# Two dK stores of head pairs issued from GpSimd as sixteen transfers of 8 partitions each

## The chip, the cores and the metric

The kernel runs on one core of a Trainium2 chip. The metric is the device time of one execution in microseconds (us), median over runs; the kernel before takes 1698.33 us (three runs, 1697.89 to 1698.5). Five engines matter: PE (TensorE, matmuls and transposes into PSUM), DVE (VectorE), ACT (ScalarE), POOL (GpSimd) and SP (SyncE, which here only issues transfers). Sixteen DMA engines move data between device memory and the on-chip memory of 128 partitions. A transfer is issued either from SP, into the queue that the profile calls `q1 hardware_dynamic`, or from POOL, into `q0 software_dynamic`. All queues are served by the same sixteen DMA engines. A transfer counts as landed when all sixteen have reported.

## The reference, cut to what matters

The reference is the forward pass and the gradient of one decode step: layer norm, attention of one query token over a cache of 4096 keys and values (4 batches x 32 heads x 128 channels, bf16), an output projection, and a gated feed-forward block, with residuals. It returns the forward result and the gradients of eight inputs.

```python
def _A_ref(x, k_cache, v_cache, wq, wo):
    q = (x @ wq).reshape(B, Sq, H, Dh).transpose(0, 2, 1, 3)
    scores = jnp.einsum("bhqd,bhkd->bhqk", q, k_cache) * (Dh ** -0.5)
    p = _softmax(scores, axis=-1)
    o = jnp.einsum("bhqk,bhkd->bhqd", p, v_cache)
    return o.transpose(0, 2, 1, 3).reshape(B, Sq, H * Dh) @ wo
...
h = x + _A_ref(_layernorm(x, axis=-1), A_k_cache, A_v_cache, A_wq, A_wo)
h2 = h + _B_ref(_layernorm(h, axis=-1), B_w1, B_w3, B_w2)
...
_out, _vjp = jax.vjp(_f, A_x, A_k_cache, A_v_cache, A_wq, A_wo, B_w1, B_w3, B_w2)
_grads = _vjp(grad_out)
```

What fills the time is the cache and its gradients. With one query token, the gradient of a head's keys is an outer product: dK[k, :] = dS[k] q, with dS[k] = scale * p[k] (dO . V[k] - c). The gradient of its values is dV[k, :] = p[k] dO. Each of K, V, dK and dV is 128 heads of 1 MB (4096 x 128 bf16). V is read twice, once for the forward pass and once for dS.

## The kernel before

Memory. A large tile `arena` is cut into 23 slots of 8 KB per partition and a little more, one head (1 MB) each. `Slot` hands out one slot; `Slot2` hands out two neighbouring ones, a pair of 2 MB. `give()` puts slots back, at the point of the program where it is called; who gets a slot next waits on the chip until the transfers that used it have landed. `free` and `age` make the choice: the slot that was given back longest ago is taken first. Up to `side_done` only eight pairs (`NPAIR`) are handed out as pairs.

Stages. First a forward pass over all 128 heads, which loads K and V of each head. Then a short middle part (feed-forward block, its gradients). Then the gradients of the cache: 32 heads one by one (`grad_V`, `grad_K`), and the other 96 as 48 pairs, the loop `for t in range(NT)` at the end of the kernel. A pair is two heads of the same batch; `two_heads` lays its 2 MB out as 128 rows of 16 KB, one for each partition, 64 partitions for each head.

One turn `t` of that loop, in the order of the program:

- `load_pairs` issues the load of V for pair `t + 3` or further ahead (line 1280, on SP);
- `front_pair(t + 3)` transposes V on PE (line 1298), copies it back on ACT (line 1299), forms dO . V on PE (line 1313), and `dO_pair` makes a small stationary operand on POOL (line 1290);
- `more_V` makes dV of a pair some turns ahead: `P2_pair` on POOL (line 1376), the outer product on DVE (line 1379, in `outer_pair`), and the store to `out_3` from SP (line 1389, in `grad_pair`);
- `grad_pair(out_2, t, ...)` does the same for dK: one DVE outer product (line 1379) into a fresh pair of slots, one store of 2 MB from SP (line 1389), and `give()`;
- after an odd turn `group_dS_pair` makes dS for the next two pairs on DVE (lines 1326 and 1329);
- `side` does pieces of other work: the gradients of the weights, with stores from SP (lines 1072, 1119, 1135, 1146) and a few small transfers from POOL: `dqr_bf` (line 1028), four rows of `out_1` (line 1064), four rows of `grad_out` (line 1083), four rows of `out_0` (line 1111) and `O_sb` (line 1124).

Each engine works through its own list in this order and waits for the others by semaphores. The order is written out by hand; nothing is scheduled later. A DMA issue on SP or POOL waits in the list of its engine until its data are ready, and what stands behind it waits too.

Of the kernel before, what the change touches and what calls it, by code (L numbers as in the profile page):

```python
# [21 lines left out]
SP = 32  # L22
NPAIR = 8
OLD = 9


@with_exitstack
def kernel(
# [22 lines left out]
    nc = tc.nc  # L51
    P = nc.NUM_PARTITIONS
# [5 lines left out]
    Dh = A_k_cache.shape[3]  # L58
# [6 lines left out]
    SJ = Sk // P  # L65
# [50 lines left out]
    def age(i):  # L116
        return given["n"] - given.get(i, -NSLOT)
# [7 lines left out]
    class Slot:  # L125
        def __init__(self, name, src=free):
            self.i = src[0]
            if part["B"] and src is free:
                lone = sorted((i for i in free if i not in part["pairs"]), key=age, reverse=True)
                self.i = lone[0] if name in SIDE or lone and age(lone[0]) >= OLD else max(free, key=age)  # L130
            src.remove(self.i)
# [76 lines left out]
    for i in range(2):  # L208
        t = fcon.tile([P, 64], BF16, name=f"onesw{i}")
# [4 lines left out]
    def ones_window(col):  # L214
# [11 lines left out]
                          in_=rowg[:, None, :, None].to_broadcast([P, 4, 8, 4]))  # L226
# [586 lines left out]
    def grad_V(s):  # L813
        b, h = bh_of(s)
        gv = Slot("gv")
        outer(gv.heads(), P2s.pop(s), reps["rdo", s // REP][:, s % REP, :])
        nc.sync.dma_start(out=rows_of(out_3[b, h]), in_=gv.heads())
        if s > 1:
            gv.give()
        else:  # L820
            first_gv.append(gv)
# [143 lines left out]
    with ExitStack() as c2:  # L965
# [206 lines left out]
        def replicate(nm_, i0):  # L1172
            if i0 >= NH or (nm_, i0 // REP) in reps:
                return
            K_ = 8 * B if i0 < 8 * B else P
            rows = dOrows_bf if nm_ == "rdo" else qrows_bf
            ps = psrep.tile([P, REP, Dh], FP32, tag="rep", name="rep_ps")
            for i in range(REP):
                nc.tensor.matmul(ps[:, i, :], lhsT=ident_b[0:K_, i0 + i:i0 + i + 1].to_broadcast([K_, P]), rhs=rows[0:K_, :],
                                 start=True, stop=True)  # L1180
            rt = rep_bufs[nm_][i0 // REP % 2]
            nc.scalar.copy(out=rt, in_=ps[:])
            reps[nm_, i0 // REP] = rt
# [11 lines left out]
        def P_pairs(s):  # L1195
            if s < SP and s not in P2s:
                P2s[s] = bw3.tile([P, SJ, 2], BF16, tag="P2", name="P2")
                nc.gpsimd.tensor_copy(out=P2s[s][:], in_=P_all[:, s, :, None].to_broadcast([P, SJ, 2]))
# [69 lines left out]
        def two(t):  # L1268
            s = SP + t // B * 2 * B + t % B
            return s, s + B  # L1270

        def two_heads(ap, t):
            b, h = t % B, H0 + t // B * 2
            return ap[b, h:h + 2].rearrange("h (p j) d -> (h p) (j d)", p=P // 2)

        def load_pair():
            t = npv["next"]
            npv["next"] += 1
            pV[t] = Slot2()
            nc.sync.dma_start(out=pV[t].t[:, 0:2 * SJ * Dh], in_=two_heads(A_v_cache, t))  # L1280

        def load_pairs(t):
            while npv["next"] < NT and (npv["next"] <= t or len(V2s) + 2 * len(pV) < 6 and len(Slot2.choices()) > 1
                                          and -min(Slot2.choices())[0] >= OLD - 2):
                load_pair()
# [33 lines left out]
        def group_dS_pair(g):  # L1319
            T = rows.pop("T").rearrange("p jj (c z l u a) -> p z l a c u jj", c=4, z=2, l=2, u=4, a=2)  # L1320
            t = rows.pop("t")[:, 0:4 * SJ].rearrange("p (l j) -> p l j", l=2)
            t5 = t.rearrange("p l (c u jj) -> p l c u jj", c=4, u=4)
            for l in range(2):
                for a, s in enumerate(two(2 * g + l)):
                    r_ = slice(64 * a, 64 * (a + 1))
                    nc.vector.tensor_scalar(out=t5[r_, l], in0=T[r_, 0, l, a], scalar1=c_rep[r_, s:s + 1],  # L1326
                                            scalar2=scale, op0=ALU.subtract, op1=ALU.mult)
            pdS[g] = bw3.tile([P, 2, 2 * SJ, 2], BF16, tag="dS2", name="dS2", bufs=1)
            nc.vector.tensor_tensor(out=pdS[g][:], in0=t[:, :, :, None].to_broadcast([P, 2, 2 * SJ, 2]),
                                    in1=P_two(2 * g)[:, :, :, None].to_broadcast([P, 2, 2 * SJ, 2]), op=ALU.mult)  # L1330
# [3 lines left out]
        def P_two(t, n=2):  # L1334
            return Pp["s"].b(NT * 2 * SJ).rearrange("p (t j) -> p t j", j=2 * SJ)[:, t:t + n, :]
# [20 lines left out]
        def replicate_pair(nm_, q):  # L1356
            if q >= NT // B or (nm_, "p", q) in reps:
                return
            s = SP + q * 2 * B
            K_ = 8 * B if s + 2 * B <= 8 * B else P  # L1360
            rws = dOrows_bf if nm_ == "rdo" else qrows_bf
            ps = psrep.tile([P, REP, Dh], FP32, tag="rep", name="rep_ps")
            for i in range(REP):
                for a in range(2):
                    n = s + i + a * B
                    nc.tensor.matmul(ps[64 * a:64 * (a + 1), i, :], lhsT=ident_b[0:K_, n:n + 1].to_broadcast([K_, P // 2]),
                                     rhs=rws[0:K_, :], start=True, stop=True, tile_position=(0, 64 * a))
            rt = rep_bufs[nm_][(H0 + q) % 2]
            nc.scalar.copy(out=rt, in_=ps[:])
            reps[nm_, "p", q] = rt  # L1370

        def P2_pair(t):
            if t < NT and t not in pP2:
                P_rows(t // B)
                pP2[t] = P2b[t % 2]
                nc.gpsimd.tensor_copy(out=pP2[t], in_=P_two(t, 1)[:, 0, :, None].to_broadcast([P, 2 * SJ, 2]))  # L1376

        def outer_pair(dst, col2, row):
            nc.vector.tensor_tensor(  # L1379
                out=dst.rearrange("p (j r t) -> p j r t", r=Dh // 2, t=2),  # L1380
                in0=col2[:, :, None, :].to_broadcast([P, 2 * SJ, Dh // 2, 2]),
                in1=row.rearrange("p (r t) -> p r t", t=2)[:, None, :, :].to_broadcast([P, 2 * SJ, Dh // 2, 2]),
                op=ALU.mult,
            )

        def grad_pair(out_ap, t, col2, row):
            g_ = Slot2()
            outer_pair(g_.t[:, 0:2 * SJ * Dh], col2, row)
            nc.sync.dma_start(out=two_heads(out_ap, t), in_=g_.t[:, 0:2 * SJ * Dh])
            g_.give()  # L1390

        O0, S0, S1, L, LP = 2, 21, 35, 5, 3
        gvd = {"n": 2, "t": 0}
# [1 line left out]
        def more_V(upto):  # L1395
            while gvd["n"] < min(SP, upto):
                s = gvd["n"]
                P_pairs(s)
                replicate("rdo", s - s % REP)
                grad_V(s)  # L1400
                P_pairs(s + 1)
                P_pairs(s + 2)
                gvd["n"] += 1
                if s % REP == 2 and s + 2 < SP:
                    replicate("rdo", s + 2)
                elif s % REP == 2:
                    replicate_pair("rdo", 0)
                if s >= SP - 2:
                    P2_pair(s - SP + 2)
            while gvd["t"] < NT and SP + 2 * gvd["t"] + 2 <= upto:  # L1410
                t = gvd["t"]
                P2_pair(t)
                replicate_pair("rdo", t // B)
                grad_pair(out_3, t, pP2.pop(t), reps["rdo", "p", t // B][:, t % B, :])
                P2_pair(t + 1)
                gvd["t"] += 1
                if t % B == 2:
                    replicate_pair("rdo", t // B + 1)

        def lead_V(s):  # L1420
            return 8 - 2 * min(3, max(0, s - 64) // 16)
# [6 lines left out]
        def side(s):  # L1428
            if O0 <= s < S0:
                step("o")  # L1430
            if s >= S1:
                step("s", 2)
            elif s >= O0:
                step("q")
# [41 lines left out]
        for t in range(NT):  # L1476
            s = SP + 2 * t
            load_pairs(t + LP)
            if t % B == 2:
                replicate_pair("rq", t // B + 1)  # L1480
            if t + LP < NT:
                front_pair(t + LP, lambda: side(s))
            else:
                if t + LP == NT:
                    rows_out()
                    rows_T()
                side(s)
            more_V(s + 2 + lead_V(s))
            grad_pair(out_2, t, pdS[t // 2][:, t % 2], reps["rq", "p", t // B][:, t % B, :])
            if t % 2 == 1 and t + 1 < NT:  # L1490
                group_dS_pair((t + 1) // 2)
            side(s + 1)
        step("s", 400)

# [29 lines left out]
```

## Time and profile before

| what | value |
|---|---|
| time, median of 3 runs | 1698.33 us (1697.89 to 1698.5) |
| profiled execution: span | 1696.2 us |
| outside of the span (median less span) | 2.1 us |
| busy share of the span: PE, DVE, ACT, POOL | 73%, 73%, 57%, 20% |
| moved by DMA | 707.45 MB, mean 417 GB/s |
| of it by q1 (issued from SP) | 704.94 MB |
| of it by q0 (issued from POOL) | 0.10 MB in 416 packets |
| stores of pairs (line 1389) | 96 of 2 MB, median 27.9 us from issue to landing |
| loads of pairs (line 1280) | 48 of 2 MB, median 32.1 us |

The span runs from the first to the last instruction of the profiled execution; all times below count from its start. The busy rows give each engine's share in forty equal slices, in tenths. The DMA row is the mean over the sixteen DMA engines, so one engine alone gives 1/16, or 0.06. The trace also holds a record of each DMA packet: its start, its length in time, its bytes and its queue, but not the number of its engine. A packet of 4 bytes ends each engine's share of a transfer.

### The profile page before, as it was taken

To read this page: it belongs to the slowest core of one execution; us is meant where nothing else is said; L and a number is where in the kernel's file an instruction comes from. 1 tells how busy PE (TensorE), PEld (TensorE's weight loads), DVE (VectorE), ACT (ScalarE), POOL (GpSimd) and SP (SyncE) were. 2 spreads that over 40 slices of the span, in tenths; PEclk is the share of its full clock that TensorE was granted. 3 is DMA by queue.
4 is the path that set the end of the run, shared out by engine and by line. 5 is a ranking of instruction groups with operands and counts; after the bars stand their busy time and mean duration, and the time that the engine had idled before them with its cause. 6 is when DMAs were issued, how large, how long until landed. Compare 5 with 4: busy or idle time off the path is not lost.

```text
span 1696.2 us, 37839 instructions
## 1 busy us (share of the span) xinstructions
PE 1233.4 (73%) x16228; PEld 943.4 (56%) x16228; DVE 1234.4 (73%) x1198; ACT 959.5 (57%) x1490; POOL 336.9 (20%) x583
## 2 busy tenths in 40 slices
PE   5889888888888888877876755667665666766650
PEld 4777667666677666655655544444444444444440
DVE  5989999999998997667766466575665655655683
ACT  3555544454454544677665555666665666666650
POOL 1211222222222222222231121011210102011120
PEclk8999999999999999899898689886678777676675
DMA  9999999999999999999999999999999999999995
GB/s 401 424 424 424 424 424 424 424 424 423 416 423 406 424 414 397 395 414 425 425 425 429 428 429 428 429 430 429 429 429 428 418 430 429 422 418 425 415 429 230
DMA packets 81000, 707.45 MB, mean 417 GB/s; under 512 B 8748, under 2 KB 12984, under 8 KB 15296
## 3 DMA queue, kind: packets, MB, share of 16 engines
q1 hardware_dynamic: 80416, 704.94, 99.0%
q8 instruction: 127, 2.08, 0.5%
q14 instruction: 41, 0.34, 0.0%
q0 software_dynamic: 416, 0.10, 0.0%
HBM read 422.59 MB, written 282.34 MB: 416 GB/s over the span
## 4 chain that ended last, share of the span: by engine, by line
DMA 46%; DVE 9%; PE 3%; issue 2%; ACT 1%; DVEq 0%; POOL 0%; SPq 0%; ACTq 0%
DMA out_dram<-arena 43%; DVE arena L1379 7%; DMA arena<-in_A_v_cache_dram 3%; DVE arena L806 1%; PE M_ps L472 1%; DVE arena L457 1%; PE pt_w L601 0%; ACT arena L1299 0%; ACT Pn L436 0%; DVEq L1519 0%; PE kP_ps L482 0%; DVE dPr L1326 0%; PE pt_tps L1298 0%; PE gu_ps L873 0%; PE dn_ps L904 0%
## 5 line engine op out<-in xcount | busy, mean ns | idle before, releaser
L1299 ACT COPY arena<-pt_tps 128x1024 bf16<-128x1024 bf16 x384 | 369.8, 1023 | 232.3 <-PE pt_tps L1298 231.6
L1298 PE MATMUL pt_tps<-ident_b,arena 128*128 128x128 bf16 x3072 | 308.1, 272 | 204.7 <-DMA arena<-in_A_v_cache_dram 149.4
L1298 PEld LDWEIGHTS <-arena 128*128 128x128 bf16 x3072 | 263.9, 125 | 304.2 <-DMA arena<-in_A_v_cache_dram 172.8
L1379 DVE TENSOR_TENSOR arena<-arena 128x8192 bf16<-128x8192 bf16 x48 | 212.5, 4427 | 205.1 <-DMA out_dram<-arena 202.3
L472 PE MATMUL M_ps<-arena 128*128 128x130 bf16 x4096 | 285.1, 222 | 42.9 <-DMA arena<-in_A_v_cache_dram 42.2
L457 DVE TENSOR_TENSOR arena<-arena 128x4096 bf16<-128x4096 bf16 x128 | 292.5, 2285 | 23.9 <-POOL arena L453 23.9
L472 PEld LDWEIGHTS <-arena 128*128 128x128 bf16 x4096 | 251.9, 99 | 64.0 <-DMA arena<-in_A_v_cache_dram 57.2
L1379 DVE TENSOR_TENSOR arena<-dS,arena 128x8192 bf16<-128x8192 bf16 x48 | 212.3, 4424 | 73.0 <-DMA out_dram<-arena 73.0
L364 DVE STREAM_TRANSPOSE arena<-arena 128x512 f32<-128x512 f32 (+1 forms) x321 | 250.7, 797 | 0.0
L359 ACT COPY arena<-pt_tps 128x1024 bf16<-128x1024 bf16 x128 | 129.5, 1012 | 188.9 <-PE pt_tps L358 150.5
L1376 POOL COPY arena<-arena 128x128 bf16<-128x128 bf16 x48 | 55.3, 1153 | 492.3 <-ACT arena L1353 286.3
L370 POOL TENSOR_TENSOR W<-qrep,wmask 128x128 bf16<-128x128 bf16 x128 | 120.2, 939 | 85.6 <-PE S_ps L390 70.8
L801 ACT COPY arena<-pt_tps 128x1024 bf16<-128x1024 bf16 x128 | 121.7, 1025 | 26.1 <-PE pt_tps L800 24.8
L453 POOL COPY arena<-P_all 128x64 bf16<-128x64 bf16 x128 | 32.7, 255 | 412.8 <-ACT P_all L447 409.8
L806 DVE TENSOR_TENSOR arena<-dS,arena 128x4096 bf16<-128x4096 bf16 x32 | 73.2, 2293 | 35.0 <-DMA out_dram<-arena 34.7
L800 PE MATMUL pt_tps<-ident_b,arena 128*128 128x128 bf16 x1024 | 78.5, 229 | 27.1 <-ACT arena L801 27.1
L1313 PE MATMUL dP_ps<-arena 128*32 128x512 bf16 x768 | 85.7, 484 | 7.6 <-ACT arena L1299 7.3
L800 PEld LDWEIGHTS <-arena 128*128 128x128 bf16 x1024 | 67.2, 104 | 37.5 <-issue 35.9
L447 ACT COPY P_all<-pt_P 32x64 bf16<-32x64 bf16 x256 | 52.1, 204 | 53.6 <-PE pt_P L443 51.4
L806 DVE TENSOR_TENSOR arena<-P,arena 128x4096 bf16<-128x4096 bf16 x29 | 66.4, 2295 | 19.8 <-DMA out_dram<-arena 19.8
L358 PE MATMUL pt_tps<-ident_b,arena 128*128 128x128 bf16 x1024 | 80.1, 222 | 0.0
L482 PE MATMUL kP_ps<-arena,onesw 128*32 128x512 bf16 x1024 | 79.6, 388 | 0.0
(245 smaller groups left out, 1576.5 us busy)
## 6 DMA issues: line engine op xcount, KB each, us to landing
out_dram<-arena SPq DMA_DIRECT2D x96, 2048.0 KB, 27.9
arena<-in_A_v_cache_dram SPq DMA_DIRECT2D x160, 1024.0 KB, 15.9
arena<-in_A_k_cache_dram SPq DMA_DIRECT2D x128, 1024.0 KB, 15.3
arena<-in_A_v_cache_dram SPq DMA_DIRECT2D x48, 2048.0 KB, 32.1
out_dram<-arena SPq DMA_DIRECT2D x72, 1024.0 KB, 20.2
arena<-in_A_wq_dram SPq DMA_DIRECT2D x8, 1024.0 KB, 14.4
arena<-in_B_w_dram SPq DMA_DIRECT2D x8, 896.0 KB, 15.3
out_dram<-arena SPq DMA_DIRECT2D x6, 896.0 KB, 28.4
```

The lines of the kernel that those rows point to most:

```text
L359: nc.scalar.copy(out=KT[:, c * GW:(c + 1) * GW, :], in_=pt[:])
L364: nc.vector.transpose(out=KT[:, c * w_:(c + n) * w_], in_=Kn[:, c * w_:(c + n) * w_])
L370: nc.gpsimd.tensor_tensor(out=W[:, hl], in0=qrep[:, :, s:s + 1].to_broadcast([P, 4, 32]), in1=wmask[:, hl, None, :].to_broadcast([P, 4, 32 ...
L457: nc.vector.tensor_tensor(out=PK[:, :, 0:Dh].rearrange("p j (r t) -> p j r t", t=2), in0=Ks[s].heads().rearrange("p j (r t) -> p j r t", t=2),
L472: nc.tensor.matmul(hold["M"][:], lhsT=Vn[:, j, :], rhs=PK[:, j, :], start=(j == 0), stop=(j == SJ - 1))
L800: nc.tensor.transpose(pt[:, i, :], v[:, g * GW + i, :], ident_b[:])
L801: nc.scalar.copy(out=v[:, g * GW:(g + 1) * GW, :], in_=pt[:])
L806: nc.vector.tensor_tensor(out=dst.rearrange("p j (r t) -> p j r t", t=2), in0=col2[:, :, None, :].to_broadcast([P, SJ, Dh // 2, 2]), in1=r ...
L1298: nc.tensor.transpose(pt[:, i, :], v[:, g * GW + i, :], ident_b[:])
L1299: nc.scalar.copy(out=v[:, g * GW:(g + 1) * GW, :], in_=pt[:])
L1313: nc.tensor.matmul(rows["acc"][32 * c:32 * (c + 1), :], lhsT=zt[t % B][:, 32 - m:64 - m], rhs=v[:, j0:j0 + 4, :], start=(pl == 0 and u == ...
L1379: nc.vector.tensor_tensor(out=dst.rearrange("p (j r t) -> p j r t", r=Dh // 2, t=2), in0=col2[:, :, None, :].to_broadcast([P, 2 * SJ, Dh / ...
```

## The change

A constant names two pairs, `t` = 30 and `t` = 38. For these, `grad_pair` of dK no longer issues its store from SP. It puts sixteen entries into a list `drips`. `drip(4)` takes up to four entries and issues each as a transfer of its own from POOL: 8 partitions, four apart, within a block of 32 (the first is partitions 0, 4, 8, ..., 28; the second 1, 5, ..., 29; the fifth begins the block at 32). Each transfer carries 8 rows of 16 KB, 128 KB in all. `drip(4)` is called twice in each turn, before and after `grad_pair` of dK, and does nothing when the list is empty. So the sixteen go out as four in the turn of the pair itself, eight in the next turn, and four in the one after; the pair's slots are given back after the last. DVE's outer product for the two pairs stays as it is, and so do all other transfers.

```diff
+SPLIT = (30, 38)
...
         def grad_pair(out_ap, t, col2, row):
             g_ = Slot2()
             outer_pair(g_.t[:, 0:2 * SJ * Dh], col2, row)
-            nc.sync.dma_start(out=two_heads(out_ap, t), in_=g_.t[:, 0:2 * SJ * Dh])
-            g_.give()
+            if out_ap is out_2 and t in SPLIT:
+                for r in range(P // 8):
+                    drips.append((two_heads(out_ap, t), g_, r))
+            else:
+                nc.sync.dma_start(out=two_heads(out_ap, t), in_=g_.t[:, 0:2 * SJ * Dh])
+                g_.give()
+
+        drips = deque()
+
+        def drip(n):
+            while drips and n:
+                dst, g_, r = drips.popleft()
+                r_ = slice(r // 4 * 32 + r % 4, r // 4 * 32 + 32, 4)
+                nc.gpsimd.dma_start(out=dst[r_], in_=g_.t[r_, 0:2 * SJ * Dh])
+                if r == P // 8 - 1:
+                    g_.give()
+                n -= 1
...
             more_V(s + 2 + lead_V(s))
+            drip(4)
             grad_pair(out_2, t, pdS[t // 2][:, t % 2], reps["rq", "p", t // B][:, t % B, :])
             if t % 2 == 1 and t + 1 < NT:
                 group_dS_pair((t + 1) // 2)
+            drip(4)
             side(s + 1)
```

## The prediction

> **What bounds the kernel now.** I read the page first: the DMA row, the queues, the chain, the issues.
>
> ```profile
> DMA  9999999999999999999999999999999999999995
> GB/s 401 424 424 424 424 424 424 424 424 423 416 423 406 424 414 397 395 414 425 425 425 429 428 429 428 429 430 429 429 429 428 418 430 429 422 418 425 415 429 230
> q1 hardware_dynamic: 80416, 704.94, 99.0%
> q8 instruction: 127, 2.08, 0.5%
> q0 software_dynamic: 416, 0.10, 0.0%
> DMA 46%; DVE 9%; PE 3%; issue 2%; ACT 1%; DVEq 0%; POOL 0%; SPq 0%; ACTq 0%
> out_dram<-arena SPq DMA_DIRECT2D x96, 2048.0 KB, 27.9
> ```
>
> The sixteen DMA engines are busy in every slice but the last; no other engine passes 73%. The change moves no byte fewer, so it can matter only by which DMA engine carries what, and by waits. The last slice is the interesting one: 230 GB/s. The busy times by stretch, cut around the end (length, then PE, PEld, DVE, ACT, POOL, then granted clock, DMA share, GB/s), and the packets of the last 17 us:
>
> ```profile
> 1640.00:1670.00 30.00, 8.63 (x84) 6.37 (x84) 26.68 (x11) 8.20 (x9) 3.50 (x1) 0.61 1.00 428
> 1670.00:1674.00 4.00, 0.00 (x0) 0.00 (x0) 0.00 (x0) 0.00 (x0) 0.00 (x0) 0.50 1.03 438
> 1674.00:1677.50 3.50, 0.00 (x0) 0.00 (x0) 0.00 (x0) 0.00 (x0) 0.00 (x0) 0.50 0.42 178
> 1677.50:1694.50 17.00, 0.00 (x0) 0.00 (x0) 0.00 (x0) 0.00 (x0) 0.00 (x0) 0.50 0.06 26
> DMA packets 31, 0.44 MB, mean 26 GB/s; under 512 B 4, under 2 KB 4, under 8 KB 4
> ```
>
> From 1677.5 to 1694.5 the share is 0.06, one engine of sixteen: 27 packets of 16 KB, one after another, while fifteen engines have nothing left. So the end is set by one late DMA engine, 17 us behind the rest, and not by the mean. The completion events say the same: the last store of a pair, issued at 1666.8, is reported by the first engine after 7.8 us, by the fifteenth after 10.8, by the last after 28.1. The gap between the fifteenth and the last report was 1.7 us for a transfer issued at 831, 8.3 at 1106, 13.8 at 1384, 17.3 at the end: one engine falls back steadily.
>
> **Which engine is late.** The packet records don't name engines, but they can be chained: a busy engine starts its next packet 3 to 4 ns before the recorded end of the last, and all sixteen run through the same list of q1 packets. Chained back from the end to 1119 us this gives sixteen complete lanes. The late lane has no hole; its 16 KB packets are 0.624 us apart on average from 1390 on, the others' 0.613 to 0.618 (0.607 undisturbed). The 24 packets of q8 in that time fall three each on eight lanes, never on the late one. So the lanes are two sets of eight, and the late lane is in the set without q8.
>
> **Where POOL's small transfers go.** q0 has 416 packets for 13 transfers, 32 each. In the stretch of the four-row store of `out_1` (line 1064):
>
> ```profile
> q0 software_dynamic: 32, 0.00, 2.1%
> ```
>
> Its records are 4 packets of 1 KB and 28 of 4 bytes: sixteen completions, and twelve fillers on the engines that got no row. So a transfer with fewer than sixteen rows still goes to all sixteen, one row each to the first engines, and 4 bytes to the rest. In the chained lanes the rows of all three late four-row transfers (`out_1`, `grad_out`, `out_0`) lie on the same four lanes. The first two transfers of the kernel, four rows each, show the same by another way: the 2 KB packets of both start 0, 21, 54 and 136 ns apart, modulo the 306 ns beat of the 8 KB packets around them. It does not rotate. And the four lanes are in the set without q8: the set of the late lane.
>
> [...]
>
> **The change, part by part.** *Removed:* two SP stores, 8 rows of 16 KB per engine each, so 16 rows on every engine. *Added:* 32 POOL transfers of 8 rows. By the above each puts one row on the first eight engines: 32 rows on each of these, none on the other eight. Net: +16 rows on eight engines, -16 on eight.
>
> If four rows take four lanes of the set without q8, I take it that eight rows take all eight of that set. Then the late engine gets 16 rows more: 16 x 0.62 = +9.9 us. Completions: 32 of 9 ns on each engine, less two, +0.3 us. Sum +10.2 us, all on the path, since the late lane has no hole to hide it in. The other seven of the set get 9.9 us too, but are 17 us early.
>
> Price of a row: from 0.607 (+9.7) up. The 1 KB rows of q0 took 42 to 43 ns from start to the next start, no surcharge over their length of 46, so I take none. The far end is a row of q8: its 16 KB packets took 0.88 to 0.97 us instead of 0.61; at +0.33 for each of 32 rows, 10.6 us more. The q0 row is the nearer, being a store of the same queue; I keep some of the far end above.
>
> *POOL.* The relevant rows (mean ns; then idle before):
>
> ```profile
> L1028 POOL DMA_DIRECT2D arena<-dqr_bf x4 | 2.2, 561 | 9.3 <-ACT dqr_bf L1024 9.3
> L1376 POOL COPY arena<-arena 128x128 bf16<-128x128 bf16 x48 | 55.3, 1153 | 492.3 <-ACT arena L1353 286.3 <-DVE arena L1379 205.9
> POOL arena L1376 <- ACT arena L1353: 92.4, 3, 31.5
> DVE arena L1379 <- DMA out_dram<-arena: 76.2, 21, 6.8
> ```
>
> An issue costs 0.56 us, eight in a turn 4.5 us. The copy of line 1376 is 0.29 us alone and up to 4.5 beside a DVE product, so an issue may be held as long: with two products a turn, 4.5 + 8.8 = 13.3 us, inside a turn of 15. The drip after `grad_pair` waits for that product on DVE. Behind it in POOL's list stand `dO_pair`, two turns ahead of PE, and `P2_pair`, one turn ahead of DVE. POOL waited over 92 us in this stretch of 180 (last two rows: waits between 1380 and 1560, with total, times, longest). Cost 0; with the cover gone a copy is late by one drip, 2 to 7 us, on a DVE that idles 76 us for landings.
>
> *Slots.* The pair of `t` = 30 is multiplied at 1433.5 to 1437.9; its store lands some 28 us later, at 1466. With the change the last four rows go out in turn 32 (product at 1460.6), about 1463, and land some 6 us later, as line 1064's did (5.5). So the pair comes free at much the same time, though later in the order of the program, with seven pairs circulating instead of eight for two turns. What that starves is the early engines first. The late one has 28 us of queue, and a pair is 4.9. Cost 0.
>
> **The sum.** Profiled span 1696.2 + 10.2 = 1706.4; with the 2.1 us that the median has outside of it, 1708.5 us.
>
> **Rivals.** *Late engine spared (faster).* The eight engines of an eight-row transfer don't contain the late one: because I chained wrongly, or because eight rows start elsewhere than four. Then the late engine loses 9.9 and gains 0.3, ending at 1694.9 - 9.6 = 1685.3; the loaded eight end at 1677.6 + 10.2 = 1687.8 and are last. 7.1 us less: 1691.2. What decides is on which side of the split one engine lies; for it speaks nothing in the records, against it the q8 lanes.
> *Even spread (no change).* Eight rows alternate between the halves or are cut over sixteen engines: the change then doesn't shift anything. +0.3 us, 1698.6. Against it: fillers and fixed lanes.
> *POOL or slots starve the queue (slower).* It takes over 28 us of issue delay before the late lane runs dry; the sums above give 7. If it did, two pairs at 4.9 us would come on top of the first case: 1718.
>
> [...] No run here shows a number of an engine.
>
> **How the numbers follow.** First case (late engine loaded, 1706.5 to 1713 with bounds on the row price): 0.78. The same with a starved queue: 0.02. Even spread: 0.08. Spared: 0.12. A measurement of this kernel can tell about 0.2%, 3.4 us. So slower 0.80, same 0.08, faster 0.12. For eight in ten the range holds the first case but for its far tail, and reaches down to the even spread: 1698 to 1713.
>
> **What would show it.** Right: the stretch with DMA share 0.06 at the end begins as before or some us later, and lasts beyond 1704; in it one or, before it, eight engines (share 0.5); the last reports of late stores come over 30 us after issue or some engines lie idle from 1440 on; q0 holds 32 x 32 packets more, 1440 in all, and 4.3 MB. Wrong: a last stretch of share 0.5 (eight engines) that ends before 1690 means that the late engine was spared; a tail of unchanged 17 us means even spread. A row of q0 with a length far over 0.61 us would mean that I priced it too low.

## The result and the profile after

The changed kernel takes 1748.32 us (median of 4 runs, 1746.09 to 1749.12); the kernel before takes 1698.41 us beside it (1697.89 to 1698.87). The ratio is 1.0293, with a 95% interval of 1.0278 to 1.0307: slower by 50 us, where 10 were forecast. The profiled execution took 1746.09 us, with a span of 1744.3 us. Lines of the code stand one further down: 1280, 1298, 1299, 1376 and 1379 are now 1281, 1299, 1300, 1377 and 1380. The SP store of a pair is line 1394, the new transfer is line 1403.

The rows of the page that answer to those shown of before: the mean of the sixteen DMA engines and their GB/s in forty slices of 43.6 us, the queues (packets, MB, share), the chain, and the stores of pairs.

```profile
DMA  9999999999999999999999999999999994699599
GB/s 401 424 424 424 424 423 425 424 424 424 416 423 413 421 411 397 397 425 425 425 428 426 429 429 428 430 431 429 428 429 421 429 430 185 252 423 425 208 392 403
q1 hardware_dynamic: 80128, 700.74, 96.0%
q0 software_dynamic: 1440, 4.29, 0.7%
DMA 41%; DVE 9%; ACT 3%; issue 2%; PE 2%; POOL 1%; DVEq 0%; SPq 0%; ACTq 0%; POOLq 0%
out_dram<-arena SPq DMA_DIRECT2D x94, 2048.0 KB, 27.1
```

The bytes went where they were meant to go: 1440 packets and 4.29 MB in q0, as the prediction counted. But the DMA row, which was 9 in every slice but the last, now falls to 4 and 6 after 1439 us and to 5 after 1614 us, the times of the two split pairs. In the chain, DMA lost 5 points and ACT and POOL came in. The next rows cut out the first hole, and the end of the run (length, then PE, PEld, DVE, ACT, POOL, granted clock, DMA share, GB/s).

```profile
1435.00:1450.00 15.00, 1.67 (x16) 1.52 (x17) 1.53 (x2) 0.15 (x1) 2.44 (x6) 0.57 0.82 348
1450.00:1463.00 13.00, 9.29 (x81) 5.61 (x80) 4.40 (x1) 10.44 (x14) 0.44 (x2) 0.71 0.42 178
1463.00:1479.00 16.00, 1.06 (x17) 0.94 (x17) 5.20 (x4) 0.00 (x0) 2.27 (x6) 0.54 0.11 45
1479.00:1500.00 21.00, 7.75 (x65) 5.45 (x65) 0.79 (x3) 8.90 (x11) 1.70 (x4) 0.54 0.75 269
...
1735.00:1744.00 9.00, 0.00 (x0) 0.00 (x0) 0.00 (x0) 0.00 (x0) 0.00 (x0) 0.50 0.73 313
```

Between 1463 and 1479 the DMA engines are at 0.11, and little else runs: PE 1.1 us of 16, DVE 5.2, ACT nothing at all. No engine is the bound there; all wait for each other. And the lone late engine of the end is gone: the last 9 us run at a share of 0.73, where before 17 us ran at 0.06. By the completion events the last report now follows the fifteenth by 0.4 us instead of 17.3. The late engine caught up while the others stood still.

Who waits for whom is in the waits (total, times, longest), first from 1380 to 1560, the stretch of the two waits shown of before, then the issues of line 1403 in POOL's timeline (start, length, what came before).

```profile
DVE arena L1380 <- DMA out_dram<-arena: 91.0, 15, 24.7
...
PE pt_tps L1299 <- ACT arena L1300: 51.1, 24, 26.6
ACT arena L1300 <- DMA out_dram<-arena: 45.1, 3, 26.7
...
POOL out_dram L1403 <- DVE arena L1380: 36.3, 2, 22.5
...
POOL out_dram L1403 <- ACT arena L1300: 19.4, 1, 19.4
```

```profile
1437.05 2.08 POOL L1403 DMA_DIRECT2D out_dram<-arena  x4 [22.53 <-DVE arena L1380]
...
1449.83 0.29 POOL L1377 COPY arena<-arena 128x128 bf16<-128x128 bf16 x1 [10.52 <-DMA out_dram<-arena]
1462.68 2.05 POOL L1403 DMA_DIRECT2D out_dram<-arena  x4 [12.56 <-ACT arena L979]
1478.46 2.05 POOL L1403 DMA_DIRECT2D out_dram<-arena  x4 [13.73 <-DVE arena L1380]
...
1500.08 2.04 POOL L1403 DMA_DIRECT2D out_dram<-arena  x4 [19.39 <-ACT arena L1300]
```

Two kinds of wait are new. ACT's copy of line 1300, which fills a slot of its own with transposed V, waits for a store to land, up to 26.7 us; in the whole run of the kernel before the trace shows no such wait of ACT. And the transfers of line 1403, whose pair was multiplied at about 1436, wait for work of ACT that has nothing to do with that pair. Four issues cost 2.04 to 2.08 us, a little under the forecast of four times 0.56, but the last of the four groups goes out 63 us after the first, where 25 were forecast. The chain of waits shows them taking turns (start, length, what).

```profile
1437.05 1.56 POOL out_dram L1403 x3
1438.60 11.18 DMA out_dram<-arena
1449.85 1.02 ACT arena L1300
...
1462.68 1.53 POOL out_dram L1403 x3
1464.21 9.31 DMA out_dram<-arena
...
```

A group of transfers lands, only then ACT or DVE may go on, and only when these are done may the next group leave. The semaphore waits that the program itself carries say the same. In the program before, these copies of ACT wait for PE and for transfers from SP that used their slot, never for one from POOL. In the changed one:

```
L1403 DMACopy    out_2 <- arena  8x8192   waits for DMAHW1, DMAHW0, DMAHW5, DVE, DMAHW6, Activation, Pool
L1300 TensorCopy arena <- pt_tps 128x1024 waits for DMASW6, DMASW7, DMASW5, DMAHW2, DMASW0, PE
L1380 TensorTensor arena <- dS, arena     waits for DMASW4, DMASW3, DMAHW4, DMASW2, DMASW1
```

(DMASW and DMAHW are the semaphores of transfers from POOL and SP.) All slots are parts of one tile, `arena`. A transfer of 8 partitions four apart, 8192 columns wide, is held by the program's own bookkeeping to touch other slots too: it waits for whoever last wrote those, and whoever writes them next waits for it. With a tile for each pair of slots these waits go, and 37.1 us with them (e6 below). These are **false waits**: nothing in the data asks for them.

### The profile page after: what moved, and what is told of

It reads as the page before. It is cut to its first block, busy times and chain, and to the rows that moved or that the text cites. A ratio compares the mean times of both kernels' runs of the same rounds, so it can differ in the third digit from the quotient of the medians.

```text
span 1744.3 us, 37916 instructions
## 1 busy us (share of the span) xinstructions
PE 1229.8 (71%) x16228; PEld 939.1 (54%) x16228; DVE 1234.0 (71%) x1198; ACT 958.8 (55%) x1490; POOL 351.6 (20%) x615
## 3 DMA queue, kind: packets, MB, share of 16 engines
q0 software_dynamic: 1440, 4.29, 0.7%
q8 instruction: 127, 2.08, 0.4%
## 4 chain that ended last, share of the span: by engine, by line
DMA 41%; DVE 9%; ACT 3%; issue 2%; PE 2%; POOL 1%; DVEq 0%; SPq 0%; ACTq 0%; POOLq 0%
DMA out_dram<-arena 39%; DVE arena L1380 8%; ACT arena L1300 2%; DVE arena L807 1%; DMA arena<-in_A_v_cache_dram 1%; PE pt_tps L1299 1%; POOL out_dram L1403 1%; ACT arena L802 0%; DVE dPr L1327 0%; DVEq L1537 0%; ACT arena L979 0%; PE dP_ps L1314 0%; PE dPT_ps L1211 0%; PE gps L985 0%; ACT arena L1370 0%
```

## The experiments

Theory W is these false waits. Against it stand P, that POOL's issues or the queue cost the time by themselves, and S, that the late engine is not among the eight that got the rows. The kernel before took 1697.9 to 1698.0 us beside them.

| run | what it is | us | ratio (95%) |
|---|---|---|---|
| changed | | 1748.32 | 1.0293 (1.0278 to 1.0307) |
| e1_contig | 8 neighbouring partitions | 1721.89 | 1.0142 (1.0127 to 1.0157) |
| e2_sp | strided, from SP | 1753.80 | 1.0330 (1.0314 to 1.0345) |
| e3_even | 16 neighbouring partitions | 1712.84 | 1.0087 (1.0072 to 1.0102) |
| e4_once | strided, sixteen at once | 1712.03 | 1.0087 (1.0070 to 1.0104) |
| e6_tiles | changed, arena in 12 tiles | 1711.26 | 1.0079 (1.0062 to 1.0096) |
| e0_tiles | before, arena in 12 tiles | 1697.67 | 1.0001 (0.9992 to 1.0010) |
| e8_tiny | 32 transfers of 8 x 128 B | 1701.88 | 1.0023 (1.0014 to 1.0032) |
| e9_hold | pairs given back later | 1700.38 | 1.0016 (1.0007 to 1.0025) |
| e5_whole | two whole stores from POOL | 1701.48 | 1.0019 (1.0009 to 1.0028) |
| e10_four | 4 rows each, late engine spared | 1700.35 | 1.0014 (1.0005 to 1.0023) |
| e11_spread | the same over four pairs | 1715.65 | 1.0102 (1.0085 to 1.0119) |

**The pattern, the queue, the count.** Four variants of the changed kernel, one thing altered in each.

e1, neighbouring partitions instead of strided ones:

```diff
-                r_ = slice(r // 4 * 32 + r % 4, r // 4 * 32 + 32, 4)
+                r_ = slice(8 * r, 8 * r + 8)
```

> Sixteen transfers of 8 neighbouring partitions each, all else as changed. Theory W (the stride of four partitions makes the program wait: each drip for everything that wrote the arena before, and everything that writes it later for the drip; no engine needs these waits): they are gone, and what is left is the predicted shift of rows to the first eight DMA engines, late one among them: 1708 us (1705 to 1713). Theory P (issuing 32 transfers from GpSimd is itself what costs): still some 1745. Theory S (waits gone, late engine spared): 1691.

e2, the same strided transfers from SP:

```diff
-                nc.gpsimd.dma_start(out=dst[r_], in_=g_.t[r_, 0:2 * SJ * Dh])
+                nc.sync.dma_start(out=dst[r_], in_=g_.t[r_, 0:2 * SJ * Dh])
```

> The strided transfers issued from SP instead of GpSimd. Theory W: the waits come from the pattern, not from the queue, so they stay, and SP's other issues now stand behind them as well: 1735 to 1790. Theory P: GpSimd no longer issues anything new: 1698 to 1710.

e3, eight transfers of 16 neighbouring partitions, two at a time:

```diff
-                r_ = slice(r // 4 * 32 + r % 4, r // 4 * 32 + 32, 4)
+                r_ = slice(16 * r, 16 * r + 16)
```

> Eight transfers of 16 neighbouring partitions for each of the two pairs, two where the change had four. One row on each of sixteen engines, so no shift between engines. Theory W: 1698.7 (1697 to 1701). Theory P, with half as many issues: some 1722. With e1 it gives the cost of the shift alone: +10 by the prediction.

e4, all sixteen strided transfers right behind the product, the pair given back at once:

```diff
                 group_dS_pair((t + 1) // 2)
-            drip(4)
+            drip(16)
```

> The strided transfers, all sixteen issued in the turn of the pair itself, after grad_pair. Theory W: one place per pair where everything waits instead of four, partly hidden in the late engine's 28 us of queue: 1708 to 1722. Theory P: as many issues, still some 1745.

The waits of e2, e4 and e1, in this order, by stretch (e2 1435 to 1520, e4 1430 to 1490, e1 1380 to 1700):

```profile
DVE arena L1380 <- DMA out_dram<-arena: 61.5, 4, 25.5
...
ACT arena L1300 <- DMA out_dram<-arena: 48.7, 3, 27.5
```

```profile
DVE arena L1380 <- DMA out_dram<-arena: 37.4, 3, 30.7
ACT arena L1300 <- DMA out_dram<-arena: 32.1, 1, 32.1
```

```profile
DVE arena L1380 <- DMA out_dram<-arena: 127.9, 29, 14.7
```

From SP the loss stays (1753.8), with the same wait of ACT: it is not the queue, and P is out. With neighbouring partitions the program carries no false wait, ACT's wait is gone from the trace, and 26 us come back. e4 keeps the waits, but meets them once for each pair instead of four times; 36 us come back although ACT stands for 32.1 us in one piece. That is the cover that the prediction spoke of: the late engine had some 28 us of queue (28.1 from issue to last report at the end of the kernel before) and worked on through the single stall, in which its lag fell from 17.0 to 1.4 us. At the end its last report follows the fifteenth by less than 0.1 us, and the time lies within 1 us of that of e6 below. As e6 also holds the pair, which costs 2.5 us by e9, the stall may still cost e4 some 3 us. In the changed kernel the stalls follow each other and use the cover up: the lag is gone by 1486, and the next stall pushes the last report of q1, compared with the kernel before at the same count of q1's bytes, from 13 to 29 us behind.

But e1 and e3 came 14 us above what W had said. The packet records show why: a 16 KB row of q0 took 613 ns on average in e4, and 682 and 709 in the two pairs of the changed kernel (611 to 616 in three of the four groups of each, 883 and 997 in the third), but 974 and 922 in e1's two pairs and 1040 and 986 in e3's. So rows of 8 or 16 neighbouring partitions were dear here; in a whole store of 128 partitions from POOL (e5 below) a row took 620 ns again. What makes a row dear no run shows. Per row that is 948 - 613 = 0.335 us (e1's mean against that of e6 below); 32 rows on the late engine make 10.7 us, and e1 less e6 is 10.6. So e1 and e3 are no clean test of "waits or none".

**The waits alone.** e6 is the changed kernel with one tile for each pair of slots. Strides, issues, bytes and the pair's release stay; only the false waits go. e0 is the control, the kernel before cut in the same way.

```diff
-    arena = slotp.tile([P, NSLOT * SLOT], BF16, name="arena")
+    arena = [slotp.tile([P, min(2, NSLOT - i) * SLOT], BF16, name=f"arena{i}") for i in range(0, NSLOT, 2)]
...
-            self.t = arena[:, self.i * SLOT:(self.i + 1) * SLOT]
+            self.t = arena[self.i // 2][:, self.i % 2 * SLOT:(self.i % 2 + 1) * SLOT]
...
-            self.t = arena[:, self.i * SLOT:(self.i + 2) * SLOT]
+            self.t = arena[self.i // 2][:, 0:2 * SLOT]
```

> The changed kernel, with the tile arena cut into twelve tiles of two slots each, so that a strided transfer can share a tile only with its own pair. False waits (theory W): the sixteen strided transfers no longer stand in the way of other slots, and what is left of the change is 16 more rows of 16 KB at 0.61 us on the first eight engines. If the late engine is among them, 1698 + 10 = 1708 (1705 to 1713), with a lone engine at the end for over 20 us, or an idle stretch that lets it catch up; if it is not, about 1691. Then no copy of line 1300 and no product of line 1380 waits for a landing of more than some us beyond the kernel before. The rival, that the GpSimd path or the held pair causes the loss whatever the waits: it stays near 1748.

> A control: the kernel before with the arena cut into twelve tiles, nothing else. Theory W holds that the cut matters only where a strided transfer reads the arena, so 1698 (1697 to 1699.5). If the cut itself helped or hurt, the loss of 37 us that left with the cut between the changed kernel (1748) and the same with twelve tiles (1711) would have to be read against this time in place of 1698.

The waits of e6 from 1435 to 1520, and its end:

```profile
DVE arena L1380 <- DMA out_dram<-arena: 38.0, 9, 12.7
```

```profile
1680.00:1690.00 10.00, 0.00 (x0) 0.00 (x0) 0.00 (x0) 0.00 (x0) 0.00 (x0) 0.50 1.01 431
1690.00:1706.00 16.00, 0.00 (x0) 0.00 (x0) 0.00 (x0) 0.00 (x0) 0.00 (x0) 0.50 0.08 34
```

The control stays at 1697.67, so the cut costs nothing by itself, and what it takes off the changed kernel is the false waits: 1748.32 - 1711.26 = 37.1 us. No copy of ACT waits for a store any more. The lone late engine is back, 16 us at 0.08, and it ends 12 us later than in the kernel before. That is the prediction's first case, as it was written, within its range. The completion events follow it: over the first split pair the last report of q1 is pushed back by 10.0 us against the kernel before at the same count of q1's bytes, where the 16 rows of that pair that each of the first eight engines gets make 9.8 at 613 ns.

**Which engine is late.** e7, a probe and not a version of the change: the kernel before in twelve tiles, with twelve extra loads from POOL in each of four turns, of 4, 5, 6 and 7 strided rows into a pair that nobody reads.

```diff
+PROBE = {16: 4, 24: 5, 32: 6, 40: 7}
...
+            if t in PROBE:
+                pr = Slot2()
+                for r in range(12):
+                    r_ = slice(r // 4 * 32 + r % 4, r // 4 * 32 + r % 4 + 4 * PROBE[t], 4)
+                    nc.gpsimd.dma_start(out=pr.t[r_, 0:2 * SJ * Dh], in_=two_heads(A_v_cache, t)[r_])
+                pr.give()
```

> A probe of which engine is late, not of the change: the kernel before with the arena cut into twelve tiles, and in the turns 16, 24, 32 and 40 twelve extra loads from GpSimd of 4, 5, 6 and 7 rows of 16 KB (V, strided partitions, into a pair that nobody reads). Transfers of k rows put one row on each of the first k engines. By the prediction's chained lanes the late engine is not among the first four: its lag behind the fifteenth report stays on its slow slope in turn 16, and jumps by 12 x 0.61 = 7.3 us in the turn from which k includes it (24: it is the fifth; 32: the sixth; 40: the seventh), less what idle time gives back; no jump at all if it is the eighth or later. The extra loads move 12 x 22 rows, 4.3 MB: 10 us more for the mean engine.

One profiled execution, 1725.37 us. While the loads of 4 rows ran (issued 1194 to 1205), the late engine's reports kept their spacing, 5.05, 5.06 and 4.85 us for two stores and a load. While the loads of 5 rows ran (1343 to 1355), they came 7.74, 7.92 and 6.35 us apart: 7.1 us more, where 12 rows make 7.4. The loads of 6 and of 7 rows push it back again, by 7.3 and 7.4 us against the kernel before at the same count of q1's bytes, and at the end it is 27.4 us behind, which is the whole loss of the run (1725.37 - 1697.98). So the late engine gets the fifth row of a transfer, and it sets the end. It is in the first eight and not in the first four, as the chained lanes had it, and S is out.

**Without bytes, without split.** e8 keeps the 32 transfers and the late release, but SP stores columns 64 and up of the two pairs in their own turn, and the transfers carry columns 0 to 63 alone (128 B rows); at that width the program carries no false wait. e9 is e0 without any transfers from POOL that only holds the two pairs as long. e5 is the kernel before with the two stores issued whole from POOL.

```diff
+                nc.sync.dma_start(out=two_heads(out_ap, t)[:, 64:], in_=g_.t[:, 64:2 * SJ * Dh])
...
-                nc.gpsimd.dma_start(out=dst[r_], in_=g_.t[r_, 0:2 * SJ * Dh])
+                nc.gpsimd.dma_start(out=dst[r_, 0:64], in_=g_.t[r_, 0:64])
```

> The changed kernel, but SP stores columns 64 to 8191 of the two pairs in their own turn, and the 32 transfers from GpSimd carry only columns 0 to 63 (8 rows of 128 B). As many issues on GpSimd, the pair held as long, but no bytes shifted between the engines, and by the program's waits none of the transfers overlaps another slot. False waits (theory W): 1698.5, 1697 to 1701. The rival, that GpSimd's issues or the pair that is held two turns longer cost time by themselves: over 1705, up to 1748 if they are all of it.

```diff
             nc.sync.dma_start(out=two_heads(out_ap, t), in_=g_.t[:, 0:2 * SJ * Dh])
-            g_.give()
+            if out_ap is out_2 and t in (30, 38):
+                held.append((g_, t + 2))
+            else:
+                g_.give()
...
+            if held and held[0][1] == t:
+                held.popleft()[0].give()
             grad_pair(out_2, t, pdS[t // 2][:, t % 2], reps["rq", "p", t // B][:, t % B, :])
```

> The kernel before with twelve tiles; all stores whole from SP as before, only the pairs of t = 30 and 38 are given back two turns later, in the place where the changed kernel gives them back. It tells what of the 3.9 us of the run with 32 small transfers (1701.9) is the held pair. If the held pair: 1701 to 1702.5. If GpSimd's issues and their packets: 1697 to 1699.5.

```diff
-            nc.sync.dma_start(out=two_heads(out_ap, t), in_=g_.t[:, 0:2 * SJ * Dh])
+            (nc.gpsimd if out_ap is out_2 and t in (30, 38) else nc.sync).dma_start(out=two_heads(out_ap, t), in_=g_.t[:, 0:2 * SJ * Dh])
```

> The kernel before, with the two dK stores of t = 30 and 38 issued whole, 128 partitions each, from GpSimd in place of SP. No split, no stride. Theory W: as before, 1697 to 1700.5. The rival, that bytes of the software queue are dear by themselves, or that SP's order matters: rows at 0.98 us in place of 0.61 would add 8 rows x 2 x 0.37 = 6 us to every engine, 1704, and rows at 1.6 us or a queue that runs dry would give 1715 or more.

The held pair costs 1700.38 - 1697.92 = 2.5 us, between its two expectations and nearer to that of the held pair; issues and tiny packets add 1701.88 - 1700.38 = 1.5 us at most, about what the intervals of the two runs leave open. So e8 came out 0.9 us above what W allowed it, far below the 1705 of its rival. The waits of e9 from 1380 to 1700 point to where the holding bites: the longest wait of DVE for a landing is 10.5 us, against 7.1 in the kernel before (second row).

```profile
DVE arena L1379 <- DMA out_dram<-arena: 105.7, 29, 10.5
```

```profile
DVE arena L1379 <- DMA out_dram<-arena: 101.9, 26, 7.1
```

e5 lies 3.5 us above before, 1 us beyond what W allowed. Its rows took 620 ns on average, so they weren't dear, and if they fell eight to an engine, as the prediction counts them from SP, none moved from one engine to another; what the 3.5 us are stays open.

**A version with the late engine spared.** What the runs say together is that 4-row transfers miss the late engine (its reports stayed 4.85 to 5.06 us apart beside them in e7). Two versions use this, both made from e0. e10 sends 64 and 48 partitions of the two pairs so, SP stores the rest; e11 spreads as many rows over four pairs, issues all of a pair in its turn and gives it back at once.

```diff
+FOUR = {30: 64, 38: 48}
...
+            k = FOUR.get(t, 0) if out_ap is out_2 else 0
+            for r in range(k // 4):
+                drips.append((two_heads(out_ap, t), g_, r, k))
+            nc.sync.dma_start(out=two_heads(out_ap, t)[k:], in_=g_.t[k:, 0:2 * SJ * Dh])
...
+                r_ = slice(r // 4 * 16 + r % 4, r // 4 * 16 + 16, 4)
```

> The late engine spared on purpose: twelve tiles; of the dK pairs of t = 30 and 38, the first 64 and 48 partitions go out from GpSimd in 16 and 12 transfers of 4 strided rows, which reach only the first four engines (the probe showed the late engine to be the fifth); SP stores the other 64 and 80 partitions, 4 and 5 rows for each engine. By theory the late engine loses 7 rows of 0.614 us, -4.3 us, and the first four gain 28 - 7 = 21 rows, +12.9 us, on a lead of 17.3: both end at 1694. Added to it what issues and the held pair cost by themselves, up to 3.9 us: 1693 to 1698. If the lag of the late engine isn't what sets the end, or the first four are not the same as in the probe: 1698 to 1702 or later.

```diff
-FOUR = {30: 64, 38: 48}
+FOUR = {26: 32, 30: 32, 34: 32, 38: 16}
...
-            drip(4)
             grad_pair(out_2, t, pdS[t // 2][:, t % 2], reps["rq", "p", t // B][:, t % B, :])
...
-            drip(4)
+            drip(8)
```

> The version that the runs so far point to: rows taken off the late engine without holding a pair. Twelve tiles; of the dK pairs of t = 26, 30, 34 and 38 the first 32, 32, 32 and 16 partitions go out from GpSimd in transfers of 4 strided rows, all of a pair in its own turn, and the pair is given back in that turn, as in the kernel before; SP stores the rest. The late engine again loses 7 rows, -4.3 us, the first four gain 21, +12.9 on a lead of 17.3. If the held pair was what ate the gain of the run before (2.5 us of the 4.3 in the run that only held it): 1694 to 1696.5. If longer packets beside the software queue's rows ate it (672 ns in place of 614 there, 3 us for each engine over the whole run): 1697 to 1700, with a small lag at the end all the same.

The ends of the two, e10 first:

```profile
1680.00:1690.00 10.00, 0.00 (x0) 0.00 (x0) 0.00 (x0) 0.00 (x0) 0.00 (x0) 0.50 0.28 118
1690.00:1694.00 4.00, 0.00 (x0) 0.00 (x0) 0.00 (x0) 0.00 (x0) 0.00 (x0) 0.50 0.06 25
```

```profile
1690.00:1700.00 10.00, 0.00 (x0) 0.00 (x0) 0.00 (x0) 0.00 (x0) 0.00 (x0) 0.50 0.26 113
1700.00:1712.00 12.00, 0.00 (x0) 0.00 (x0) 0.00 (x0) 0.00 (x0) 0.00 (x0) 0.50 0.06 26
```

In e10 the balance worked: the lone stretch shrank to 4 us, the lag from 17.3 to 2.3 us. The time didn't follow (1700.35, above its 1693 to 1698). The trace is of its fastest execution, 1696.66 us; even there the last report fell back by 2.5 us against the kernel before at the same count of q1's bytes, so that under 2 of the 4.3 us were left. What ate the gain isn't separated. The pairs are held (2.5 us in e9), the issues cost up to 1.5 us, and q1's 16 KB packets that ran beside the 4-row transfers took 672 and 681 ns on average, where most take 611. The last can't be charged to the time as it stands, since e6 has the same (665 and 686 ns) and its loss is nearly all rows and held pair.

In e11 no pair is held, and it is slower by 18 us, far outside both expectations: there the held pair is not the cause. The packets beside its transfers took 716 to 755 ns. Summed over the last 340 us, what q1's 16 KB packets took above 611 ns is 4 us for each engine in the kernel before, 8 in e10 and in e6, and 16 in e11. The late engine itself fell back in e11 by some 20 us at the same count of q1's bytes, in four steps of 4 to 6 us, one at each of the four pairs. Longer packets can make such steps; so could rows of its own, since eight rows at 613 ns are 4.9 us, if in this execution the late engine was one of the first four. The probe ran once, in another execution, and no run tells the two apart. Why packets grow beside POOL's stores of few rows is open too; beside the loads of e7 they took 618 to 630 ns. No kernel here beats the one before.

## Why the prediction was wrong

**The shift of rows held.** 32 rows against 16, all on the first eight engines, the late one among them, 0.62 us each, nothing hidden: +10.2 predicted. With the false waits away (e6) the loss is 13.3 us, of which 16 x 0.613 = 9.8 are the rows and 2.5 the held pair (e9); the 1.0 left is within what issues and packets can cost (e8 less e9, 1.5). The chained lanes, the fixed first engines and the price of a q0 row, taken from the q0 records instead of the dearer q8 ones, were all right for the strided rows of e6. A dear row like the one kept for the far end of the range exists, but not for the reason given: rows of 8 or 16 neighbouring partitions cost 0.92 to 1.04 us (e1, e3), while the queue as such does not (620 ns in e5).

**The step that failed** is the pricing of the new waits at nothing, in the parts on POOL and on slots. It took for granted that "the drip after `grad_pair` waits for that product on DVE", and nothing else, and that nobody waits for a drip but the one who gets its pair next. Both were read out of the meaning of the code. The program's waits came from footprints in a tile, and there a strided transfer over one big tile overlapped other slots. That is +37.1 us of the 50: it is measured as the changed kernel less e6, with e0 as control. The sum is 37.1 (false waits) + 9.8 (rows) + 2.5 (held pair) = 49.4, against 49.9 measured. The first term is itself what e6 leaves of the loss, so the sum tests only the other two. The held pair, also priced at nothing under slots, is the smaller miss.

**The starved queue.** The third rival had the right place and nearly the right threshold: "over 28 us of issue delay before the late lane runs dry". e4 shows that threshold at work, where a stall of 32 us in one piece left a time within 1 us of that of e6, which has none of these waits. It was given 0.02, because the delay was worked out as 7 us from issue times alone; it was four stalls in a row, with ACT waiting up to 26.7 us for landings. Its price, 1718, was too low for the same reason.

**What it said to look for.** q0 holds 1440 packets and 4.3 MB: right. Engines idle from 1440 on: they were, but the prediction named it as a sign of its first case, and here it came from starvation. A lone stretch that lasts beyond 1704: wrong for the changed kernel, since the late engine caught up in the stalls, right for e6. POOL's copies late by a drip: one copy of line 1377 was late by 10.5 us, but it waited for a landing, a wait of the new kind, and not for an issue. The issues were nearly harmless, 1.5 us or less (e8 less e9). Direction and bound were right; the size was wrong by the one mechanism that no view of the old trace shows, and that had no bound in the sum.

## What to carry to other kernels

The transfers with a new access pattern brought waits of their own here, both ways, and 37.1 us with them; before pricing such a transfer at nothing, ask whose storage its footprint covers in the tile, and put one landing (here 10 to 28 us) for each group of issues as the far end of the cost. Tiles cut to pairs of slots kept such footprints apart (e6) and cost nothing by themselves (e0, 1697.67 us). And the lead of the other engines over the late one was cover: one stall of 32.1 us fitted into it for some 3 us (e4), four in a row didn't (the changed kernel).

## What was not expected of the hardware

A 16 KB row of q0 took 613 ns on average from partitions four apart in e4 and e6 (682 and 709 in the two pairs of the changed kernel), 0.92 to 1.04 us from 8 or 16 neighbours (e1, e3), and 620 ns in a whole store (e5). One engine's lag, built up over hundreds of us (1.7 us for a transfer issued at 831 of the kernel before, 13.8 for one at 1384), went away within one stall (17.0 to 1.4 us between the completions at 1450 and 1494 in e4): the late engine still had queue to work on. Removing the lag by other means bought no time in e10. And packets of the main queue became longer while POOL's stores of few rows ran beside them (665 to 755 ns on average in e6, e10 and e11, where most take 611), but hardly beside its loads (618 to 630 ns in e7).
